# Attention with a routed mixture of experts on one core: the router's first choice queued one pair after its logits, the expert's number computed earlier in its round, half of the first expert's first matrix asked for after the first tokens are turned, and two penalty steps of round 0 on VectorE

## The chip, the core and the metric

The kernel runs on one core of a Trainium2 chip. The metric is the device time of one execution in microseconds (us). The engines have short names in the profile: PE is TensorE (its weight loads are PEld), DVE is VectorE, ACT is ScalarE, POOL is GpSimd and SP is SyncE. Each works through its own instructions in a fixed order and waits on semaphores. Here SP issues the plain DMAs, and GpSimd the indirect ones (gathers and scatters of rows).

## The reference

```python
# q, k, v: (8 batches, 8 heads, 576 positions, 64), fp32
scores = q @ k.T / sqrt(64) + bias(head, distance), inside a causal window of 128
x = (softmax(scores) @ v) as (4608 tokens, 512)
# mixture of experts: 8 experts, each takes at most cap = 576 tokens
logits = x @ w_gate                       # (4608, 8)
for idx in argsort(-logits.flatten()):    # greedy, best pair first
    tok, e = idx // 8, idx % 8
    if assigned[tok] < 0 and counts[e] < cap:
        assigned[tok] = e; counts[e] += 1
for e in range(8):
    out[assigned == e] = relu(x[assigned == e] @ w1[e]) @ w2[e]
```

## The kernel before

**Attention** (`attention`, L26). The work goes over 32 pairs of heads (4 pairs in each of 8 batches), in a software pipeline that is written out by hand: the loop at L316 has, for each `n`, the weights' minima of pair n-1 (`least`, DVE, L133) and their exponentials (`exps`, ACT), the transposes of pair n-2 on PE (`turn`, L157) with copies out of PSUM (`turned`, the tiles `PT`, L165), attention times values of pair n-3 (`av`, tile `x`, L53), and the end of pair n-4: `copy_out` (ACT, and one small GpSimd copy `xT<-xT`, L215), `natural` (PE, weights `wn`, tiles `pt`), and `divide` (DVE: a reciprocal `rs` at L240, shares of the logits `Lp` at L248, the output `xb` at L255). All of these are kept in program order on their engines. After the last pair of a batch, `logits` (L287) adds the shares up on GpSimd in four small adds (L296 to L299) into `L_sb`; for the last batch DVE does it itself (L291).

**The router** (`Router`). It replaces the greedy loop by eight rounds: in each one the expert that fills up first is settled, by counting how many candidates lie above each of 64 thresholds. Its work of round 0 is spread over the attention part as steps (generators): `first_choice` (best expert of each token, two steps: `b`, `ne`, `cand`, and then `am`, `OH`), put on a list by `early` (L595), and, after batch 5, `early_counts` (L618: `ext`, `em`, `ed`, then `ev` to `hi`, then `w` to `kq`, then the indicators `ind` and PE's counts). `early_step` (L607) runs one step a pair, at L363, behind `divide`. Since they are issued through a helper, these instructions all have line 442 in the profile (L446 in the changed program). The rest of round 0 (`phase`, L647) follows the attention: its results are `ei` (the expert's number, as an integer) and `idx` (the rows of its tokens).

**The handover** (`layer_moe`, L979). GpSimd gathers the first expert's tokens by `idx` (`g`, five gathers, L840). SP reads `ei` into a register and loads the first weight matrix in four quarters of 512 KB (`raw`, L822): three (`SOON`) at once, the last one after `late`, a copy of `ei` on DVE that is queued behind the first step of round 1. PE runs `WARM0` = 10 matmuls on zeros (L848) to be kept busy, then turns the tokens (`turn`, L851: tiles `pg` and `po` on PE, `xh` on ACT, `xl` on DVE) with `WARM1` = 4 matmuls on zeros behind each of the first two groups. Each quarter is split into a rounded part and the rest (`split`, L825: a cast `hl` on ACT, L829, and two subtractions on DVE, L831).

**The experts.** For each of eight experts: `layer1` (tile `ph`, L887, then relu on ACT and the rest on DVE) and `layer2` (tile `po`, L912 to L915), and a scatter of the rows by GpSimd. Expert 0 goes over the first 256 tokens for all eight column blocks, and then over the others; blocks 0 and 1 need quarter 0 of the matrix, blocks 2 and 3 quarter 1, and so on, 12 matmuls a block and token group. `slot` puts the next round's steps, weight loads, splits and gathers between the matmuls. From L984 on a scheduler sets the order on each engine, and `tc.issue_after(i)` only says that what is issued in the block stands behind instruction `i` on its own engine. In each round but the last, the candidates of the settled expert are struck out (`L2`, `Lt`, `L1` at L756 to L759, on GpSimd), and round k+1 begins with `first_choice` on the result.

Of the kernel before, what the change touches and what calls it, by code (L numbers as in the profile page):

```python
# [5 lines left out]
F32 = mybir.dt.float32  # L6
F32R = mybir.dt.float32r
BF = mybir.dt.bfloat16
I32 = mybir.dt.int32
AF = mybir.ActivationFunctionType  # L10
ALU = mybir.AluOpType
# [8 lines left out]
NT = N // 128  # L20
# [5 lines left out]
def attention(tc, pools, qk_in, v_in, rel_in, C, x_dram, L_sb, router):  # L26
# [289 lines left out]
    for n in range(NPAIRS + LAG + 2):  # L316
# [42 lines left out]
        if ends:  # L359
            divide(k - 2, N)  # L360
            if (k - 2) % NP == NP - 1 and k - 2 < NPAIRS - 1:
                logits((k - 2) // NP)
            router.early_step(room if turns else None)  # L363
        if 0 <= k - 1 < NPAIRS - 1:
            av(k - 1)
        if n < NPAIRS:
            scores(n, 1)
# [39 lines left out]
CONST_AT = 4  # L407
WARM, WARM0, WARM1 = 11, 10, 4
EARLY = 4
AHEAD = (18, 0, 0)  # L410
EARLY0 = 1
SOON, HI0 = 3, 1
W_LOAD = [(0, 1, 0, 0), (0, 1, 1, 2), (0, 1, 2, 6), (0, 1, 3, 10),
# [17 lines left out]
def bc(ap, shape):  # L431
    return ap.to_broadcast(shape)
# [17 lines left out]
class Router:  # L450
# [144 lines left out]
    def early(self, c0, c1):  # L595

        choice = self.first_choice(self.L0, self.b0, self.am0, self.OH0, c0, c1)
        if c1 == NT:
            for steps in self.steps + [choice]:
                for _ in steps:  # L600
                    pass
            return
        self.steps.append(choice)
        if c1 == FIRST:
            self.steps.append(self.early_counts())
# [12 lines left out]
    def early_counts(self):  # L618
# [6 lines left out]
        for i in range(EARLY_CUTS):  # L625
            a, z = (c1 * j // EARLY_CUTS for j in (i, i + 1))
            self.indicate(ind, key, a, z)
            if i % 2 == 1:
                yield
        cnt = self.count(ind, self.OH0, 0, c1)  # L630
# [16 lines left out]
    def phase(self, k, exact=False):  # L647
# [48 lines left out]
        nc.vector.scalar_tensor_tensor(keyv, Dc, float(CAP), self.left, ALU.is_ge, ALU.mult)  # L696
        nc.vector.tensor_reduce(mx, keyv, AX.X, ALU.max)

        m = rt.tile([128, NT], BF, name="m")
# [8 lines left out]
        nc.tensor.matmul(sp[:, 0:NT], self.C["tri"], m, start=False, stop=True)  # L708
        ef = self.small("ef")
        nc.vector.tensor_scalar(ef, mx, 1.0, -1.0, ALU.max, ALU.mult)  # L710
        ei = self.ei[k] = rt.tile([128, 1], I32, name="ei", bufs=4)
        nc.vector.tensor_scalar(ei, ef, 8.0, None, ALU.add)
        hi = self.small("hif", NT)
# [37 lines left out]
        if k < 7:  # L751
# [3 lines left out]
            L2 = rt.tile([128, 8, NT], F32, name="L2", bufs=1)  # L755
            self.tc.nc.gpsimd.tensor_tensor(L2, L, bc(self.pen.unsqueeze(2), [128, 8, NT]), ALU.add)  # L756
            Lt = rt.tile([128, 8, NT], F32, name="Lt", bufs=1)
            self.tc.nc.gpsimd.tensor_scalar(Lt, T1, 100.0 * BIG, 1.0, ALU.mult, ALU.mult)
            self.tc.nc.gpsimd.tensor_tensor(self.L1, Lt, L2, ALU.add)  # L759
        ov = self.small("ov")  # L760
# [50 lines left out]
class MoE:  # L811
# [39 lines left out]
    def turn(self, gs, first=False):  # L851
# [6 lines left out]
        for h, (g, r) in enumerate(gs):  # L858
# [6 lines left out]
            if first and h < TURN0 - 1:  # L865
                self.keep_warm(WARM1)
            nc.scalar.copy(xh[:, :, 128 * h:128 * h + r], ps[:, :, :r])  # L867
            nc.vector.tensor_tensor(xl[:, :, 128 * h:128 * h + r], ps[:, :, :r],  # L868
                                    xh[:, :, 128 * h:128 * h + r].bitcast(F32), ALU.subtract)
# [109 lines left out]
def layer_moe(tc, P, C, r, x, w1, w2, out, exact):  # L979
# [4 lines left out]
    with tc.issue_after(r.last.ins):  # L984
        for _ in range(EARLY0):
            next(route)
        late = P["rt"].tile([1, 1], I32, name="late")
        last = tc.nc.vector.tensor_copy(late, r.ei[0][0:1, 0:1])
    raw += list(m.loads(late, 0, range(SOON, 4)))
    W = {(0, 0): [m.split(raw[c]) for c in range(HI0)]}  # L990
# [4 lines left out]
    with tc.issue_after(m.last.ins):  # L995
        for _ in range(TURN0):
            next(tn)
# [130 lines left out]
```

## Time and profile before

| what | value |
|---|---|
| median of 3 runs | 739.1 us (739.07 to 739.36) |
| the profiled execution | 739.65 us |
| its span, first to last instruction | 737.8 us |
| PE busy | 682.8 us, 93% |
| PE weight loads busy | 599.2 us, 81% |
| DVE busy | 468.0 us, 63% |
| ACT busy | 331.4 us, 45% |
| POOL busy | 154.5 us, 21% |
| granted clock of PE, mean | 0.971 |
| moved by DMA | 92.74 MB |

The profile is one execution. The attention part fills the first 236 us or so, the rest of round 0 and the handover go to about 267 us, and the experts have what follows. In the timeline a row is: start, duration, engine, line, operation, out<-in, shape, count, and in brackets how long the engine stood idle before it and what ended that. In a table of windows each row is a stretch: its length, the busy time and the instructions of PE, PEld, DVE, ACT and POOL, the granted clock of PE, the busy share of the DMA engines and GB/s. The router's instructions in attention are told apart by their tiles, since all have line 442.

### The profile page before, as it was taken

To read this page: it belongs to the slowest core of one execution; us is meant where nothing else is said; L and a number is where in the kernel's file an instruction comes from. 1 tells how busy PE (TensorE), PEld (TensorE's weight loads), DVE (VectorE), ACT (ScalarE), POOL (GpSimd) and SP (SyncE) were. 2 spreads that over 40 slices of the span, in tenths; PEclk is the share of its full clock that TensorE was granted. 3 is DMA by queue.
4 is the path that set the end of the run, shared out by engine and by line. 5 is a ranking of instruction groups with operands and counts; after the bars stand their busy time and mean duration, and the time that the engine had idled before them with its cause. 6 is when DMAs were issued, how large, how long until landed. Compare 5 with 4: busy or idle time off the path is not lost.

```text
span 737.8 us, 19156 instructions
## 1 busy us (share of the span) xinstructions
PE 682.8 (93%) x7416; PEld 599.2 (81%) x7417; DVE 468.0 (63%) x1854; ACT 331.4 (45%) x990; POOL 154.5 (21%) x340
## 2 busy tenths in 40 slices
PE   7989889899897479999999999999999999999992
PEld 4888788788786268889878989988988988989981
DVE  6767678677777788969768847856865625423200
ACT  6878788688785152424223324314224324322200
POOL 4111221121212121323123132132033022011010
PEclk9999999999999599999999999999999999999996
DMA  8465465455522360815326135135134325201010
GB/s 298 136 201 170 139 194 170 156 174 173 154 84 81 112 203 1 290 60 183 131 88 228 44 130 157 58 124 174 60 115 148 117 93 169 76 29 36 1 36 32
DMA packets 35140, 92.74 MB, mean 126 GB/s; under 512 B 3808, under 2 KB 13152, under 8 KB 35040
## 3 DMA queue, kind: packets, MB, share of 16 engines
q1 hardware_dynamic: 29152, 72.55, 30.0%
q0 software_dynamic: 5888, 18.88, 7.8%
q8 instruction: 60, 0.98, 0.6%
q14 instruction: 40, 0.33, 0.1%
HBM read 72.54 MB, written 18.87 MB: 124 GB/s over the span
## 4 chain that ended last, share of the span: by engine, by line
PE 78%; DVE 13%; DMA 3%; POOL 2%; issue 2%; ACT 1%; SPq 0%; POOLq 0%; DVEq 0%; ACTq 0%
PE ph L887 25%; PE po L912 10%; PE po L913 10%; PE po L915 8%; PE s L53 6%; PE pt L53 5%; PE pt L157 4%; DVE u L133 4%; PE x L53 4%; PE pg L864 2%; PE m L575 1%; DMA craw<-in_cst_dram 1%; DVE PT L165 1%; DMA g<-x,idx 1%; DMA qk<-in_qk_dram 1%
## 5 line engine op out<-in xcount | busy, mean ns | idle before, releaser
L887 PE MATMUL ph<-xh,hl 128*128 128x288 f32 (+2 forms) x1024 | 191.8, 299 | 0.0
L887 PEld LDWEIGHTS ph<-xh,hl 128*128 128x128 f32 x1024 | 154.5, 189 | 1.0
L144 ACT ACTIVATE u<-u,mn 128x192 f32<-128x192 f32 (+2 forms) x288 | 123.9, 433 | 33.9 <-DVE mn L133 33.9
L912 PE MATMUL po<-hl,hh 128*128 128x512 f32 x320 | 129.4, 404 | 0.0
L913 PE MATMUL po<-hl,hh 128*128 128x512 f32 x320 | 124.9, 390 | 0.0
L887 PE MATMUL ph<-xl,hl 128*128 128x288 f32 (+2 forms) x512 | 115.8, 297 | 0.0
L893 ACT ACTIVATE hh<-ph 128x288 fp32r<-128x288 f32 (+2 forms) x128 | 46.4, 409 | 149.8 <-PE ph L887 140.8
L133 DVE CUSTOM_DVE_ANT_0 u<-s,bm 128x192 f32<-128x192 f32 x308 | 86.4, 333 | 41.2 <-PE s L53 40.7
L915 PE MATMUL po<-hl,hlo 128*128 128x512 f32 x256 | 100.3, 392 | 0.0
L831 DVE TENSOR_TENSOR hl<-raw,hl 128x512 fp32r<-128x512 f32 x128 | 85.4, 688 | 14.9 <-ACT hl L829 13.4
L928 POOL DMA_INDIRECT out_dram<-o,idx x40 | 44.5, 1112 | 204.6 <-ACT o L923 115.8
L887 PEld LDWEIGHTS ph<-xl,hl 128*128 128x128 f32 x512 | 84.2, 189 | 0.0
L868 DVE TENSOR_TENSOR xl<-pg,xh 128x512 fp32r<-128x512 f32 (+1 forms) x37 | 23.7, 640 | 84.7 <-ACT xh L867 84.5
L898 DVE SCALAR_TENSOR_TENSOR hlo<-ph,hh 128x288 fp32r<-128x288 f32 (+2 forms) x128 | 49.5, 417 | 40.8 <-ACT hh L893 40.0
L829 ACT CAST hl<-raw 128x1024 fp32r<-128x1024 f32 x64 | 65.5, 1049 | 19.7 <-DMA raw<-in_w_dram 14.7
L53 PE MATMUL s<-qk 64*64 64x192 f32 (+1 forms) x1112 | 70.1, 326 | 2.0 <-DVE mn L133 1.7
L157 PE MATMUL pt<-ident_sb,u 128*128 128x128 f32 x368 | 54.2, 282 | 17.0 <-DVE PT L165 15.6
L912 PEld LDWEIGHTS po<-hl,hh 128*128 128x128 f32 x320 | 60.2, 188 | 11.5
L913 PEld LDWEIGHTS po<-hl,hh 128*128 128x128 f32 x320 | 60.3, 188 | 11.1
L157 PEld LDWEIGHTS pt<-ident_sb,u 128*128 128x128 f32 x368 | 39.1, 140 | 27.7 <-DVE PT L165 18.4
L923 ACT COPY o<-po 128x512 f32<-128x512 f32 x31 | 18.2, 587 | 88.2 <-PE po L915 53.4
L840 POOL DMA_INDIRECT g<-x,idx x40 | 42.9, 1073 | 68.7 <-PE pg L864 33.8
(218 smaller groups left out, 951.9 us busy)
## 6 DMA issues: line engine op xcount, KB each, us to landing
raw<-in_w_dram SPq DMA_DIRECT2D x64, 512.0 KB, 3.5
qk<-in_qk_dram SPq DMA_DIRECT2D x32, 576.0 KB, 4.8
v<-in_v_dram SPq DMA_DIRECT2D x32, 288.0 KB, 3.4
x<-xb SPq DMA_DIRECT2D x14, 512.0 KB, 3.5
x<-xb SPq DMA_DIRECT2D x8, 128.0 KB, 3.0
x<-xb SPq DMA_DIRECT2D x4, 256.0 KB
g<-x,idx POOLq DMA_INDIRECT x40
out_dram<-o,idx POOLq DMA_INDIRECT x40
```

What stands on the lines that cost most here:

```text
L53: put(nc.tensor.matmul(out, w, a, start=start, stop=stop, skip_group_check=True))
L133: put(nc.vector.tensor_tensor_reduce(out=u[rows], in0=x[rows, c:c + 64 * m].rearrange("q (j k) -> q j k", k=64), in1=bm[n % NP][rows, y:y ...
L144: put(nc.scalar.activation(u, u, AF.Exp, bias=st["mn"][:, i:i + 1], scale=-1.0, accum_out=st["sm"][:, i:i + 1]))
L157: put(nc.tensor.transpose(ps[:, c:c + 128], u[:, o + 128 * j:o + 128 * j + 128], ident))
L829: self.last = nc.scalar.copy(hl[:, 0, :], raw)
L831: nc.vector.tensor_tensor(hl[:, 1, c:c + 512], raw[:, c:c + 512], hl[:, 0, c:c + 512].bitcast(F32), ALU.subtract)
L887: nc.tensor.matmul(pp[t], w[:, a, j, fo:fo + 128], x[:, j, cut[t]:cut[t + 1]], start=(j == 0 and a == 0 and x is xh), stop=(j == 3 and a = ...
L893: nc.scalar.activation(o, pp[t], AF.Relu)
L898: nc.vector.scalar_tensor_tensor(d, pp[t][:, c0:c1], 0.0, o[:, c0:c1].bitcast(F32), ALU.max, ALU.subtract)
L912: nc.tensor.matmul(po, a, wh, start=(f == 0), stop=False)
L913: nc.tensor.matmul(po, a, wl, start=False, stop=(f == 7 and t == 4))
L915: nc.tensor.matmul(po, hl[:, f, 128 * t:128 * t + 128], wh, start=False, stop=(f == 7))
```

## The change

1. `early` puts an empty step in front of each batch's `first_choice`, so the choice begins one pair after its logits were added up; all router steps behind it move by a pair too. From pair 32 of the loop on, the step runs behind `av` and not before it, and twice where nothing is turned any more. `early_counts` issues its three indicators in one step.
2. `ef` and `ei` stand directly behind `kmx`, before `m`.
3. In round 0 the penalties `L2` and `L1` are computed on DVE, `L1` in one operation without `Lt`. The other rounds are as before.
4. `SOON` is 2: two quarters are loaded by `ei`, the other two by `late`, which now stands behind the first turned tokens (`m.turned`, an `xl`). `WARM0` is 16.

```diff
-            router.early_step(room if turns else None)
+            if n < NPAIRS:
+                router.early_step(room)
         if 0 <= k - 1 < NPAIRS - 1:
             av(k - 1)
+        if n >= NPAIRS:
+            for _ in range(1 if turns else 2):
+                router.early_step(room if turns else None)
...
-WARM, WARM0, WARM1 = 11, 10, 4
+WARM, WARM0, WARM1 = 11, 16, 4
...
-SOON, HI0 = 3, 1
+SOON, HI0 = 2, 1
...
-        self.steps.append(choice)
+        self.steps += [iter([None]), choice]
...
             self.indicate(ind, key, a, z)
-            if i % 2 == 1:
-                yield
...
         nc.vector.tensor_reduce(mx, keyv, AX.X, ALU.max)
+        ef = self.small("ef")
+        nc.vector.tensor_scalar(ef, mx, 1.0, -1.0, ALU.max, ALU.mult)
+        ei = self.ei[k] = rt.tile([128, 1], I32, name="ei", bufs=4)
+        nc.vector.tensor_scalar(ei, ef, 8.0, None, ALU.add)
...
-        ef = self.small("ef")
-        nc.vector.tensor_scalar(ef, mx, 1.0, -1.0, ALU.max, ALU.mult)
-        ei = self.ei[k] = rt.tile([128, 1], I32, name="ei", bufs=4)
-        nc.vector.tensor_scalar(ei, ef, 8.0, None, ALU.add)
...
-            self.tc.nc.gpsimd.tensor_tensor(L2, L, bc(self.pen.unsqueeze(2), [128, 8, NT]), ALU.add)
-            Lt = rt.tile([128, 8, NT], F32, name="Lt", bufs=1)
-            self.tc.nc.gpsimd.tensor_scalar(Lt, T1, 100.0 * BIG, 1.0, ALU.mult, ALU.mult)
-            self.tc.nc.gpsimd.tensor_tensor(self.L1, Lt, L2, ALU.add)
+            eng = nc.vector if k == 0 else self.tc.nc.gpsimd
+            eng.tensor_tensor(L2, L, bc(self.pen.unsqueeze(2), [128, 8, NT]), ALU.add)
+            if k == 0:
+                nc.vector.scalar_tensor_tensor(self.L1, T1, 100.0 * BIG, L2, ALU.mult, ALU.add)
+            else:
+                Lt = rt.tile([128, 8, NT], F32, name="Lt", bufs=1)
+                eng.tensor_scalar(Lt, T1, 100.0 * BIG, 1.0, ALU.mult, ALU.mult)
+                eng.tensor_tensor(self.L1, Lt, L2, ALU.add)
...
-            nc.vector.tensor_tensor(xl[:, :, 128 * h:128 * h + r], ps[:, :, :r],
+            self.turned = nc.vector.tensor_tensor(xl[:, :, 128 * h:128 * h + r], ps[:, :, :r],
...
         for _ in range(EARLY0):
             next(route)
-        late = P["rt"].tile([1, 1], I32, name="late")
-        last = tc.nc.vector.tensor_copy(late, r.ei[0][0:1, 0:1])
-    raw += list(m.loads(late, 0, range(SOON, 4)))
...
     tn = m.turn(g, True)
     with tc.issue_after(m.last.ins):
-        for _ in range(TURN0):
+        next(tn)
+
+    with tc.issue_after(m.turned.ins):
+        late = P["rt"].tile([1, 1], I32, name="late")
+        last = tc.nc.vector.tensor_copy(late, r.ei[0][0:1, 0:1])
+    raw += list(m.loads(late, 0, range(SOON, 4)))
+    with tc.issue_after(m.last.ins):
+        for _ in range(TURN0 - 1):
             next(tn)
```

On DVE in attention, at the end of the pair whose batch has just been completed, and of the pair behind it (`L442` and `L446` are the helper's line before and after the change):

```order
 L255 TENSOR_TENSOR xb<-pt,rs 128x2x128
-L442 TENSOR_REDUCE b_73<-L_sb 128x4
-L442 TENSOR_TENSOR ne<-L_sb,b_73 128x8x4
-L442 SCALAR_TENSOR_TENSOR cand<-ne,c_eb 128x8x4
 L133 ISA u,mn<-s,bm_300 128x3x64
...
 L255 TENSOR_TENSOR xb<-pt,rs 128x2x128
-L442 TENSOR_REDUCE am_75<-cand 128x4
-L442 TENSOR_TENSOR OH_76<-c_eb,am_75 128x8x4
+L446 TENSOR_REDUCE b_73<-L_sb 128x4
+L446 TENSOR_TENSOR ne<-L_sb,b_73 128x8x4
+L446 SCALAR_TENSOR_TENSOR cand<-ne,c_eb 128x8x4
 L133 ISA u,mn<-s,bm_119 128x2x64
```

The three ops that read `L_sb` have left the pair in which it is written and stand where `am` and `OH` stood; those two stand one pair further on.

On GpSimd at the handover, before the change (`g` are the gathers, `L_4822` is `L2` and `L_72` is `L1`):

```order
L215 COPY xT<-xT 128x64 x2
L758 TENSOR_SCALAR Lt<-T_4754 128x288
L840 DMA g<-x,idx 128x512
L756 TENSOR_TENSOR L_4822<-L_sb,pen 128x288
L840 DMA g<-x,idx 128x512
L759 TENSOR_TENSOR L_72<-Lt,L_4822 128x288
L840 DMA g<-x,idx 128x512 x2
L840 DMA g<-x,idx 64x512
```

and after it:

```order
L219 TENSOR_SCALAR sd<-sm 128x8
L222 TENSOR_SCALAR sd<-sm 64x1 x4
L215 COPY xT<-xT 128x64 x2
L846 DMA g<-x,idx 128x512 x4
L846 DMA g<-x,idx 64x512
L764 TENSOR_SCALAR Lt<-T_5283 128x288
```

The five gathers stand together, with nothing of round 0 between them.

On DVE at the same place, after the change, from `idx` to the second group of turned tokens (`hl` are the splits' subtractions, `L_72` is `L1`):

```order
L446 TENSOR_TENSOR L_4822<-L_sb,pen 128x288
L837 TENSOR_TENSOR hl<-raw,hl 128x512
L446 SCALAR_TENSOR_TENSOR L_72<-T_4754,L_4822 128x288
L446 TENSOR_REDUCE ov<-Dc 128x1
L837 TENSOR_TENSOR hl<-raw,hl 128x512
...
L837 TENSOR_TENSOR hl<-raw,hl 128x512
L493 SCALAR_TENSOR_TENSOR cand<-ne,c_eb 128x288
L874 TENSOR_TENSOR xl<-pg,xh 128x4x128
L495 TENSOR_REDUCE am<-cand 128x36
L1003 COPY late<-ei 1x1
L874 TENSOR_TENSOR xl<-po,xh 128x4x128
```

Before, `late` stood behind `left` and one `ov`, ahead of all splits; now it stands behind four subtractions (two quarters) and the first `xl`.

## Prediction

> **What bounds the kernel now.** I first read the span and asked which waits TensorE (PE) has in the attention part. The columns are total, times, longest, in us; the rows are PE's own longest wait and the waits that stand behind it on VectorE (DVE).
>
> ```profile
> span 737.8 us, 19156 instructions
> ...
> PE pt L157 <- DVE PT L165: 15.6, 12, 2.1
> ...
> DVE b L442 <- POOL L_sb L299: 5.4, 3, 1.8
> DVE b L442 <- POOL L_sb L298: 4.6, 3, 1.5
> ```
>
> PE loses 15.6 us waiting for DVE copies (`PT`), and DVE itself stands 10.0 us, in six places, before the first op of `first_choice` (`b`), whose logits GpSimd has not yet added up. The timeline shows one of the six.
>
> ```profile
> 187.66 1.58 PE L53 MATMUL x<-PT,v 64*64 64x64 f32 x68
> ...
> 192.34 0.23 DVE L442 TENSOR_REDUCE b<-L_sb 128x5 f32<-128x40 f32 x1 [1.81 <-POOL L_sb L299]
> 192.37 0.24 POOL L215 COPY xT<-xT 128x64 f32<-128x64 f32 x1
> ...
> 192.66 0.30 PEld L53 LDWEIGHTS pt<-wn_sb,xT 128*128 128x128 f32 x2 [0.26 <-POOL xT L215]
> 192.84 0.21 DVE L442 SCALAR_TENSOR_TENSOR cand<-ne,c_eb 128x40 bf16<-128x40 bf16 x1
> ...
> 195.31 0.44 PE L157 MATMUL pt<-ident_sb,u 128*128 128x128 f32 x2 [2.14 <-DVE PT L165]
> ...
> 196.67 2.73 PE L53 MATMUL x<-PT,v 64*64 64x64 f32 x68
> ```
>
> DVE stands 1.81 us, then does 0.7 us of choice (192.34 to 193.05); everything queued behind it on DVE is late by that sum, the `PT` copy too, and PE stands 2.14 us. Then the same 68 matmuls take 2.73 us in place of 1.58. The windows say why; the column after POOL is PE's granted clock. The first eight windows run from one `rs` reciprocal (L240, one a pair) to the second after it: six that hold a stall, two that hold none.
>
> ```profile
> 46.52:62.67 16.15, 14.16 (x255) 12.68 (x254) 10.97 (x62) 11.32 (x45) 3.56 (x16) 0.89 0.49 153
> 75.65:91.38 15.73, 13.28 (x278) 11.70 (x276) 10.95 (x62) 11.19 (x45) 3.68 (x16) 1.00 0.49 157
> 103.85:119.00 15.15, 12.93 (x255) 11.42 (x254) 10.90 (x62) 11.19 (x45) 3.56 (x16) 1.00 0.52 163
> 131.98:148.59 16.61, 14.43 (x277) 13.04 (x276) 11.04 (x60) 11.27 (x45) 3.67 (x16) 0.90 0.46 149
> 161.06:176.19 15.13, 12.92 (x255) 11.42 (x254) 10.88 (x60) 11.19 (x45) 3.55 (x16) 1.00 0.52 164
> 189.18:205.78 16.60, 14.41 (x263) 12.57 (x265) 11.22 (x64) 11.31 (x45) 3.67 (x16) 0.90 0.47 150
> 91.38:103.85 12.47, 12.47 (x260) 11.46 (x258) 9.86 (x57) 11.07 (x45) 2.37 (x12) 1.00 0.59 187
> 119.00:131.98 12.98, 12.98 (x273) 11.54 (x272) 10.12 (x57) 11.08 (x45) 2.38 (x12) 1.00 0.57 180
> ...
> 196.90:200.20 3.30, 3.30 (x82) 3.22 (x76) 2.92 (x17) 2.54 (x10) 1.08 (x6) 0.50 0.03 7
> ```
>
> Two plain pairs take 12.7 us on the mean, with PE busy throughout; two with a stall take 15.1 to 16.6. The six sum to 95.4, six plain ones to 76.4: 19.0 us of excess. Three of the six have the clock at half for a while (0.89, 0.90, 0.90), and are on the mean 1.1 us longer than the three at 1.00.
>
> The other loss is the handover to the experts, the last part that I read.
>
> ```profile
> 250.91 0.15 DVE L442 TENSOR_SCALAR ei<-ef 128x1 int32<-128x1 f32 x1
> ...
> 252.10 18.47 SPq L822 DMA_DIRECT2D raw<-in_w_dram  x8
> ...
> 254.60 3.92 PE L848 MATMUL ph<-zero 128*128 128x512 bf16 x9 [0.22 <-issue]
> ...
> 254.84 0.33 DVE L442 SCALAR_TENSOR_TENSOR idx<-ia 64x5 int32<-64x5 f32 x2
> ...
> 256.14 1.19 POOL L840 DMA_INDIRECT g<-x,idx  x1 [7.05 <-DVE ov L442]
> 257.36 0.92 POOL L756 TENSOR_TENSOR L<-L_sb,pen 128x288 f32<-128x288 f32 x1
> 259.69 0.80 POOL L759 TENSOR_TENSOR L<-Lt,L 128x288 f32<-128x288 f32 x1
> 262.09 1.11 PE L864 MATMUL pg<-ident_sb,g 128*128 128x128 f32 x4 [3.57 <-DMA g<-x,idx]
> 264.25 0.68 DVE L868 TENSOR_TENSOR xl<-pg,xh 128x512 fp32r<-128x512 f32 x1
> 266.02 1.05 ACT L829 CAST hl<-raw 128x1024 fp32r<-128x1024 f32 x1
> 266.67 0.72 PE L887 MATMUL ph<-xh,hl 128*128 128x256 f32 x4
> 268.20 1.89 DVE L831 TENSOR_TENSOR hl<-raw,hl 128x512 fp32r<-128x512 f32 x3
> ```
>
> The first gather is issued at 256.14 and its tokens are there at 262.09, 5.95 us later; PE, warmed until about 259, stands 3.57 us, and the first expert matmul follows at 266.67.
>
> ```profile
> 257.90:261.70 3.80, 0.62 (x2) 0.00 (x0) 2.11 (x4) 1.27 (x2) 3.37 (x4) 0.95 0.91 290
> 261.70:265.10 3.40, 3.01 (x10) 1.86 (x11) 3.40 (x9) 0.59 (x1) 2.37 (x2) 0.50 0.83 275
> 487.90:489.60 1.70, 1.70 (x9) 1.39 (x8) 0.23 (x1) 0.00 (x0) 1.00 (x1) 1.00 0.00 0
> ```
>
> While that gather flies, the DMA engines are 91% busy with weights, and after PE's wait the clock is at half for 3.4 us. The third row holds a lone gather of a later expert: nothing moves for 1.70 us after its issue, so its 256 KB, at the 290 GB/s of the first row, would be there after about 2.6 to 3.
>
> **The change part by part.** *First choice one pair later.* In the pair after the logits the step is now empty, and GpSimd has a whole pair (over 6 us) for the adds that DVE waited 1.81 us for. DVE's wait goes in all six places, and with it the 2.1 us waits of PE after which the clock fell. What stays: the same five ops of choice, 0.7 us for the three shown and at most as much for the other two, on a DVE that PE waits for, so 0.6 to 1.1 us an event; and a wait that DVE's stall has covered so far. GpSimd's `xT` copy (192.37) still stands behind the four adds, and PE's last two `wn` weight loads wait for it until 192.66. They would have come at about 191.9; but PE's next work needs a `PT` copy, which without the stall could be done at 192.7, so this costs some 0.25 us, at most 0.8. I take 1.2 us of 3.2 as staying: 6 x 1.2 = 7.4, so 11.6 of 19.0 go. Bounds: all but 0.6 an event goes, 15.4; or 0.8 and 1.1 stay and the half clock too (3 x 1.1 = 3.3), 19.0 - 11.4 - 3.3 = 4.3.
>
> The Trainium skill ("TensorE: Matmul & The Clock Gate", "What's actually happening") has the clock halved after an idle window of about 3.4 us. Here a wait of 2.14 us sufficed, so the measurement decides; by the page's rule the stall would not be the cause, 3.3 us of half clock would stay, and the time would be 727.4.
>
> *The other router steps move one pair later too.* Of them `w` to `kq` leaves a pair in which PE waits for DVE, for one after the last scores.
>
> ```profile
> 221.03 0.20 DVE L442 TENSOR_SCALAR w<-hi,lo 128x1 f32<-128x1 f32 x1
> ...
> 222.36 0.31 DVE L442 TENSOR_SCALAR kq<-c,lo,rw 128x52 bf16<-128x52 f32 x1
> ...
> 230.57 0.32 PE L442 MATMUL pt<-OH,ind 128*128 128x16 bf16 x5 [0.32 <-DVE ind L442]
> ```
>
> That is 1.6 us of DVE (221.03 to 222.67), and the 0.32 us for which PE stood before `av` goes because counts now follow `av`. From the sum of 1.9 I take 1.5, since 1.6 us of DVE may push the `PT` copies of pair 31; bounds 0 and 1.9. Folding the indicator steps together removes a step and no work.
>
> *Expert number sooner.* Its two small ops stand before `m` in place of behind `ex`: three DVE ops stand no longer before `ei`, which I put at half a microsecond, and `idx` comes some 0.3 later (two dependent ops of 0.15, as the `ei` row), so the gather would be issued at 256.45 in old time.
>
> *Penalties on DVE, two quarters of the weights late.* Now 1 MB and not 1.5 is on its way before the gathers, half a microsecond sooner, and the five gathers follow each other on GpSimd without the 0.92 and 0.80. The tokens are then there 2.9 us after 256.45, at 259.4; at worst as now, 262.4. PE's 16 warm-up matmuls, 0.436 us each at half clock (3.92 for 9), begin at 254.9 and end at 261.9 if the clock never rises, at 260.0 if half of them run at full. I take 260.9 for the first transposes: here the warm-ups, not the gather, decide. From there to the first expert matmul before took 4.58 us (262.09 to 266.67), 3.0 of them at half clock; at full clock about 3.4. So 264.3 in place of 266.7: 2.4 us. Bounds: 260.0 and 3.1 give 263.1, 3.6 gained; 262.4 and 4.6 give 267.0, 0.3 lost.
>
> The cover for the late quarters:
>
> ```profile
> raw<-in_w_dram SPq DMA_DIRECT2D x64, 512.0 KB, 3.5
> ...
> 271.15 5.47 PE ph L887 x44
> ```
>
> The first `xl` (2.16 us behind its transposes at half clock) starts at about 262.3 and ends at 263.0, `late` follows after one op (put at 0.6, as one of the three subtractions) at 263.6, the DMA is issued 1.2 later, as after `ei` (250.91 to 252.10), and lands 3.5 later, at 268.3; cast 1.05, the first half's subtraction 0.63: the third quarter is usable at 270.0. PE needs it after 48 matmuls of 0.124 us, at 270.3. The slack is 0.3 us; a landing of 5 us would cost 1.2. SP's queue is held by `late` until then, and behind it only second-layer loads stand, which aren't needed before some 23 us of layer 1. PE's waits inside the first expert I expect about 0.5 us longer, since its counts of the next round now stand earlier in PE's row; bounds -0.6 and 1.9, one subtraction less or three more in front of them.
>
> The Trainium skill ("SBUF — State Buffer", "Who interferes with whom") speaks against this edit: GpSimd, which writes a gather's descriptors, is locked out of their shared port by some DVE instructions, and DVE now has more to do at this point. The gather of 256.14 took 1.19 us and the lone one 1.00 (busy POOL in its window): 0.2 us at most, and the rule stays as a rival.
>
> **The sum.** -11.6 - 1.5 - 2.4 + 0.5 = -15.0 us. The profiled execution took 739.65 us (span 737.8 and 1.85 around it), which gives 724.65; the median of the runs is 0.55 lower, 739.1, so 724.1.
>
> **The rivals.** (1) *The handover gives nothing:* the warm-ups stay cold, or the third quarter comes 2 to 3 us late. For it: a slack of only 0.3 us. Against: 91% busy DMA was what held the gather. 739.1 - 11.6 - 1.5 + 0.5 = 726.5, chance 0.14. GpSimd held off by DVE, by one 0.63 us subtraction for each of the first three gathers, gives 726.0; chance 0.04. Half clock that comes in attention without the stall, 3.3 us, gives 727.4; chance 0.03, since the three longest events are those that have it. (2) *The wait moves to GpSimd:* PE stands the whole 0.8 us for `xT` in each event, and the clock still falls. For it: 0.26 us of that wait is in the trace. Against: it's at most a third of the 2.14 us after which the clock fell. The gain of the first edit becomes 4.3 to 8: 739.1 - 6 - 1.5 - 1.9 = 729.7; chance 0.07. (3) *Slower:* PE starves in the first expert's first layer while it waits for late quarters, and its clock stays at half, as it did from 261.70 to 265.10. A window of 3.4 us at half costs 1.7 us of PE's work, so it decides from nine windows in a row, 15.3 us, which gives 739.4 and more with PE's waits on top, 741. The layer is long enough (192 matmuls at 0.124 us, 24 us at full clock); but PE would have to stand much of every window, and only two quarters are late. Chance 0.01. (4) *It doesn't do what it says:* the steps are kept in program order, and the order shows them moved; 739, chance 0.01. The forecast has 0.70.
>
> **How the numbers follow.** Forecast 724.1, its own range 720.5 to 727.5 (the handover's bounds and 0.4 us an event). Rival 2 widens it upward to 730; downward, 15.4 and 3.6 both coming give 719. I say 719.5 to 730. About 0.2% (1.5 us) is what a measurement of this kernel can tell from no change: faster 0.97, same 0.015, slower 0.015.
>
> **What would show it.** Right: no DVE wait for `L_sb`; windows over two pairs after logits of 13.5 to 14.3 us at clock 1.00; the first expert matmul 2.4 us nearer to `idx`; the first gather there within 3.5 us. Wrong: PE waits for `xT` of over 0.5 us, clock under 1 in attention, PE waits for `hl` in the first layer, or warm-ups that end after the gather has landed by more than 2 us.

## The result, and the profile after

The kernel after the change takes 721.7 us (median of 4 runs, 721.6 to 722.3), the kernel before, beside it on the same chip, 739.2 us (4 runs): a ratio of 0.9765, 95% interval 0.9748 to 0.9781, 17.5 us less. The profiled execution took 722.27 us. Single executions of the kernel before, in the rounds of the experiments below, lie between 737.2 and 743.9 us (mean granted clock 0.975 and 0.964), so a difference of one or two us between two of them says little.

The waits in the attention part, in the same columns as before (total, times, longest, in us):

```profile
core 0 of [0], span 720.5 us
...
PE pt L157 <- DVE PT L165: 6.2, 14, 0.9
...
PEld pt L53 <- POOL xT L215: 0.8, 3, 0.3
```

DVE's waits for `L_sb` are gone from the list. PE's wait for `PT` copies fell from 15.6 to 6.2 us, the longest from 2.1 to 0.9. No row has PE itself waiting for GpSimd's `xT`; only its weight loader does, 0.8 us in all.

One of the six places in the timeline of after, the pair that now holds the first half of the choice:

```profile
188.19 0.22 DVE L446 TENSOR_REDUCE b<-L_sb 128x5 f32<-128x40 f32 x1
...
188.69 0.21 DVE L446 SCALAR_TENSOR_TENSOR cand<-ne,c_eb 128x40 bf16<-128x40 bf16 x1
...
191.02 0.44 PE L157 MATMUL pt<-ident_sb,u 128*128 128x128 f32 x2 [0.51 <-DVE PT L165]
...
192.38 1.58 PE L53 MATMUL x<-PT,v 64*64 64x64 f32 x68
```

The choice no longer waits, costs the 0.71 us of its three ops (188.19 to 188.90), and PE stands 0.51 us in place of 2.14; the 68 matmuls behind take 1.58 us again, not 2.73.

The windows of after, cut at the same reciprocals (the first six rows: the two pairs behind each of six batches' logits; the last two: the next two pairs behind the first two of these); the column behind POOL is PE's granted clock:

```profile
47.87:61.08 13.21, 12.70 (x255) 11.42 (x254) 10.51 (x60) 11.09 (x45) 3.53 (x16) 1.00 0.62 187
74.39:88.00 13.61, 13.05 (x277) 11.68 (x276) 10.53 (x60) 11.18 (x45) 3.66 (x16) 1.00 0.59 181
100.82:114.02 13.20, 12.69 (x255) 11.41 (x254) 10.50 (x58) 11.08 (x45) 3.53 (x16) 1.00 0.60 187
127.34:140.95 13.61, 13.06 (x278) 11.68 (x276) 10.53 (x60) 11.18 (x45) 3.65 (x16) 1.00 0.59 181
153.77:166.97 13.20, 12.69 (x255) 11.41 (x254) 10.49 (x58) 11.08 (x45) 3.53 (x16) 1.00 0.58 188
180.29:193.90 13.61, 13.05 (x277) 11.68 (x276) 10.53 (x60) 11.17 (x45) 3.66 (x16) 1.00 0.58 182
61.08:74.39 13.31, 13.05 (x273) 11.54 (x272) 10.42 (x59) 11.07 (x45) 2.35 (x12) 1.00 0.56 175
88.00:100.82 12.82, 12.56 (x260) 11.46 (x258) 10.18 (x57) 11.07 (x45) 2.36 (x12) 1.00 0.57 182
```

The six sum to 80.4 us against 95.4, all at clock 1.00. The last two, plain before, now hold the choice's second half, and each took 0.34 us more than before. An event is therefore counted over three pairs below: 134.0 us before for the six, 120.8 after.

The handover in after (timelines of DVE, PE, GpSimd and the DMA queue):

```profile
237.57 0.15 DVE L446 TENSOR_SCALAR ei<-ef 128x1 int32<-128x1 f32 x1
...
242.16 5.35 PE L854 MATMUL ph<-zero 128*128 128x512 bf16 x15 [0.22 <-issue]
...
242.39 0.33 DVE L446 SCALAR_TENSOR_TENSOR idx<-ia 64x5 int32<-64x5 f32 x2
...
243.69 1.18 POOL L846 DMA_INDIRECT g<-x,idx  x1 [22.18 <-ACT hl L835]
...
247.34 0.60 PE L870 MATMUL pg<-ident_sb,g 128*128 128x128 f32 x4
...
249.75 0.13 DVE L1003 COPY late<-ei 1x1 int32<-1x1 int32 x1
...
250.66 2.34 SPq L828 DMA_DIRECT2D raw<-in_w_dram  x4
...
250.75 0.60 PE L893 MATMUL ph<-xh,hl 128*128 128x256 f32 x3
...
256.02 1.29 DVE L837 TENSOR_TENSOR hl<-raw,hl 128x512 fp32r<-128x512 f32 x2
```

The first transposes start 3.65 us behind the first gather's issue (5.95 before), with no gap between them and the warm-ups, and the first expert matmul 3.41 us later (4.58 before). The late quarters are issued at 250.66, and the third is split from 256.02 on; PE shows no wait for it.

Where the 17.29 us of the two spans went, stage by stage (us, from the timelines; a minus is time gained):

| stage | predicted | measured |
|---|---|---|
| six events, three pairs each | -11.6 | -13.2 |
| last pairs, to the last logits sum | -1.5 | -0.9 |
| `idx` later / gather to transposes / transposes to first expert matmul | -2.4 | +0.3 - 2.3 - 1.2 = -3.2 |
| experts, to the end | +0.5 | -1.4 |
| up to the first pair's reciprocal | 0 | +1.4 |

The last row belongs to that one execution: there is nothing of the change in that stretch, and the start of the other kernels' profiles below varies by as much. The four rows of the change add up to -18.7, against -15.0 in the forecast.

### The profile page after: what moved, and what is told of

Read it like the earlier page. It is cut to its first block, busy times and chain, and to the rows that moved or that the text cites. A ratio compares the mean times of both kernels' runs of the same rounds, so it can differ in the third digit from the quotient of the medians.

```text
span 720.5 us, 19162 instructions
## 1 busy us (share of the span) xinstructions
PE 678.5 (94%) x7422; PEld 595.2 (83%) x7423; DVE 466.9 (65%) x1856; ACT 330.6 (46%) x990; POOL 155.2 (22%) x337
## 4 chain that ended last, share of the span: by engine, by line
PE 80%; DVE 14%; DMA 2%; issue 1%; SPq 0%; ACT 0%; POOL 0%; POOLq 0%; DVEq 0%; ACTq 0%
PE ph L893 28%; PE po L918 10%; PE po L919 10%; PE po L921 8%; PE s L53 6%; DVE u L133 5%; PE pt L53 5%; PE pt L157 4%; PE x L53 3%; PE pg L870 2%; DVE xb L255 2%; PE m L579 1%; DMA craw<-in_cst_dram 1%; DVE PT L165 1%; PE ph L854 1%
## 5 line engine op out<-in xcount | busy, mean ns | idle before, releaser
L837 DVE TENSOR_TENSOR hl<-raw,hl 128x512 fp32r<-128x512 f32 x128 | 85.0, 683 | 14.3 <-ACT hl L835 13.9
L846 POOL DMA_INDIRECT g<-x,idx x40 | 44.8, 1120 | 82.0 <-PE pg L870 33.9
L921 PEld LDWEIGHTS po<-hl,hlo 128*128 128x128 f32 x256 | 48.0, 188 | 10.6
```

Of the source, the lines that this page charges most:

```text
L837: nc.vector.tensor_tensor(hl[:, 1, c:c + 512], raw[:, c:c + 512], hl[:, 0, c:c + 512].bitcast(F32), ALU.subtract)
L921: nc.tensor.matmul(po, hl[:, f, 128 * t:128 * t + 128], wh, start=False, stop=(f == 7))
```

## The experiments

My theory: nearly all of the gain is the wait that DVE no longer has for GpSimd's sum, with the PE waits and the half clock that follow from it (some 13.5 us); the handover brings some 3. Rivals: the choice is merely in a better place, the wait did not matter; or the handover and the clock carry the gain; or DVE's new work holds off GpSimd's gathers and hides a larger gain.

All the runs in one table; before is the median beside them on the same chip. "Events" is the sum over six times three pairs; then the times from the first gather's issue to the first transposes, from these to the first expert matmul, and from this to the last matmul, all from one profile of each kernel.

| kernel | median us | before | ratio, 95% interval | events | gather to transposes | to first matmul | experts |
|---|---|---|---|---|---|---|---|
| before | | 739.2 | | 134.0 | 5.95 | 4.58 | 457.1 |
| after | 721.7 | 739.2 | 0.9748 to 0.9781 | 120.8 | 3.65 | 3.41 | 455.8 |
| attention_alone | 724.5 | 739.5 | 0.9758 to 0.9832 | 120.9 | 5.76 | 4.86 | 456.3 |
| no_empty_step | 736.1 | 739.5 | 0.9937 to 0.9981 | 133.9 | 3.60 | 3.37 | 456.2 |
| logits_on_dve | 730.5 | 739.5 | 0.9844 to 0.9932 | 124.3 | 5.51 | 5.77 | 455.8 |
| penalties_on_gpsimd | 726.7 | 739.5 | 0.9784 to 0.9868 | 120.9 | 4.08 | 4.51 | 459.3 |
| three_quarters_first | 723.5 | 739.2 | 0.9754 to 0.9812 | 120.8 | 4.11 | 3.29 | 458.8 |
| ten_warmups | 726.2 | 739.2 | 0.9775 to 0.9838 | 120.9 | 4.13 | 4.80 | 459.0 |
| two_groups_turned | 726.0 | 739.2 | 0.9782 to 0.9842 | 120.9 | 4.03 | 2.85 | 459.7 |
| choice_once_per_two | 719.7 | 739.2 | 0.9710 to 0.9767 | 118.9 | 3.64 | 3.39 | 455.8 |
| steps_before_av | 724.7 | 739.4 | 0.9763 to 0.9828 | 120.8 | 3.59 | 3.35 | 456.7 |
| choice_once_per_three | 719.0 | 739.4 | 0.9683 to 0.9739 | 118.3 | 3.99 | 3.36 | 456.6 |
| two_inputs_beside_gathers | 725.1 | 739.4 | 0.9752 to 0.9841 | 120.9 | 3.63 | 3.38 | 458.9 |
| one_input_beside_gathers | 725.7 | 739.4 | 0.9763 to 0.9846 | 120.9 | 3.74 | 3.34 | 460.3 |

**The attention edits alone** (before with these lines of the change and nothing else):

```
-            router.early_step(room if turns else None)
+            if n < NPAIRS:
+                router.early_step(room)
...
+        if n >= NPAIRS:
+            for _ in range(1 if turns else 2):
+                router.early_step(room if turns else None)
...
-        self.steps.append(choice)
+        self.steps += [iter([None]), choice]
...
-            if i % 2 == 1:
-                yield
```

> Only the attention edits (empty step ahead of each first choice, later router steps, step behind av from pair 32 on, indicators in one step); the handover as before. My theory (the gain in attention is DVE's six waits for GpSimd, PE's waits behind them and the half clock that they bring): the attention part is 13 to 14 us shorter, the handover as before, 725.5 us (724.5 to 726.5). Rival (the handover and a better phase of the clock carry much of the 17.5 us): 729 or more.

724.5 us. Events as in after, handover as in before (GpSimd's first three gathers stand 2.4 and 2.2 us apart, PE waits for the first):

```profile
247.59 1.11 PE L866 MATMUL pg<-ident_sb,g 128*128 128x128 f32 x4 [3.30 <-DMA g<-x,idx]
```

These edits alone bring 15.0 of the 17.5 us. By the profile, 14.1 of them lie in the attention part (13.2 in the events, 0.9 in the last pairs) and 0.8 in the experts, which these edits leave alone. The handover as the carrier of the gain is out.

**The empty step alone taken away** (after with one element less):

```
-        self.steps += [iter([None]), choice]
+        self.steps.append(choice)
```

> The changed kernel without the empty step: the first choice stands again in the pair of its logits, all other edits stay. My theory: the six DVE waits, 10 us, and the half clock come back; what is left is the handover, 3.5 us, and 1.4 us of waits inside the experts: 734.3 us (733.3 to 735.5). Rival (what helps is that steps moved to cheaper places around the last pairs): 726 or less.

736.1 us, 0.6 above the expected range (the profiled execution, 734.99, lies in it). The waits of this kernel in attention are those of before, to the digit:

```profile
PE pt L157 <- DVE PT L165: 15.6, 12, 2.1
...
DVE b L446 <- POOL L_sb L299: 5.4, 3, 1.8
...
DVE b L446 <- POOL L_sb L298: 4.6, 3, 1.5
```

One empty element in a list of steps is worth 13 us; the events are back at 133.9, and three of them have windows at half clock.

**The wait taken away, the choice left in its old place** (before with the sums of all batches on DVE, as the last batch has them, so that no GpSimd result is waited for):

```
-        if b == B - 1:
+        if b >= 0:
```

> The kernel before, with the logits of every batch added up on DVE in two reductions, as the last batch has it, in place of GpSimd's four adds; the first choice stays in the same pair. My theory (it is the wait, not the place): no wait and no half clock, but 0.64 us more work on DVE in each of seven pairs and the choice's work as before; of the 19.0 us of excess some 9 to 11 remain, so 729 to 731 us, 730. Rival (it is the place: the pair of the logits can't take the choice's work): the excess stays, 736 to 739 us.

730.5 us. The events fall by 9.8 us although DVE has more to do in that pair, and the clock stays at 1.00 in attention in the profiled execution. PE's waits in that part lie between; the second fence has the last event, 23.33 us long before:

```profile
PE pt L157 <- DVE PT L165: 11.1, 15, 1.6
```

```profile
181.02:202.46 21.44, 19.38 (x390) 16.83 (x391) 17.08 (x95) 16.75 (x67) 3.56 (x18) 1.00 0.49 154
```

So most of it is the wait, not the place. What is left against after is 3.4 us. The sums that GpSimd did beside DVE are six times 0.62 us on DVE here, 3.7 us, so they could be all of it; this kernel doesn't separate them from the place of the choice.

**The penalties of round 0 back on GpSimd** (after with these two lines):

```
-            eng = nc.vector if k == 0 else self.tc.nc.gpsimd
+            eng = self.tc.nc.gpsimd
...
-            if k == 0:
+            if k < 0:
```

> The changed kernel with round 0's penalties on GpSimd again, in three operations as before. My theory (the second and third gather set the first expert matmul once the first is early): the gathers stand apart again, the third 1.6 us later, the first expert matmul 1 to 1.6 us later: 722.9 us (722.3 to 723.5). Rival (DVE's added work holds the gathers or the splits up as much as it saves): 721.7 us or less.

726.7 us, well above what I expected. The handover lost 1.5 us, as expected; the timelines of GpSimd and PE:

```profile
242.18 1.62 POOL L846 DMA_INDIRECT g<-x,idx  x1 [7.30 <-ACT hl L835]
243.84 0.68 POOL L759 TENSOR_TENSOR L<-L_sb,pen 128x288 f32<-128x288 f32 x1
244.68 1.23 POOL L846 DMA_INDIRECT g<-x,idx  x1 [0.17 <-issue]
...
246.26 0.66 PE L870 MATMUL pg<-ident_sb,g 128*128 128x128 f32 x4 [0.56 <-DMA g<-x,idx]
...
297.16 0.66 PE L870 MATMUL pg<-ident_sb,g 128*128 128x128 f32 x4 [2.08 <-DVE xl L874]
```

But the last row lies some 46 us into the experts, where the second expert's tokens are turned: there PE now waits 2.08 us, the clock falls to half behind it, and the experts take 3.5 us longer. The two edited lines do not touch this place, but the order of the instructions on DVE, ACT and PE is another there than in after. The profiles below fall into two groups, with this loss and without it.

**Three quarters of the first matrix ahead of the gathers, not two** (after with `SOON, HI0 = 3, 1`):

> After, with three quarters of expert 0's first matrix in flight ahead of the gathers instead of two. My theory (the gather lands behind the weights that are already moving): 512 KB more are ahead of it, so the first gather takes 1.6 to 2.3 us longer to the first transposes (3.65 us in after becomes 5.3 to 5.9, as the 5.76 of the run with the attention edits alone), the time is 723.2 to 724.0. Rival (only the spacing of GpSimd's descriptors matters, the bytes in flight do not): transposes stay 3.6 to 3.8 us behind the gather's issue, 721.7.

723.5 us, in my range for the wrong reason. The gather took 4.11 us to the transposes, 0.46 longer than in after and not 1.6 to 2.3, and even that is no price: ten_warmups and choice_once_per_three, with two quarters ahead, have 4.13 and 3.99. The time went in the second expert's turn, 3.0 us. My step, "1 MB and not 1.5 is on its way before the gathers", is not what freed the gather. The DMA queue's rows in before (from one window of its timeline) show what did:

```profile
256.42 2.88 SPq L822 DMA_DIRECT2D raw<-in_w_dram  x2
```

Before, a fourth and a fifth quarter were issued at 256.42 and 258.96, while the gather of 256.14 was in flight. After, and in this experiment, the queue is held by `late` until the first tokens are turned, and issues nothing in that time. So it is the place of `late`, not the number of quarters, that matters; what the earlier `ei` adds was not separated (the first quarter is issued 4.0 us ahead of the gather before, 4.9 in this experiment and in after). The gathers' closeness counts for the groups behind the first: with the penalties between them PE waited 0.51 and 0.44 us for the second and third, and the stretch to the first expert matmul was 1.1 us longer.

**Ten warm-ups, not sixteen** (after with `WARM, WARM0, WARM1 = 11, 10, 4`):

> After, with 10 warm-up matmuls of TensorE ahead of the first transposes instead of 16. In after the warm-ups ran without a gap into the transposes. My theory (warm-ups, not the gather, decide by a little): they end 1 to 2 us sooner, the transposes then come as soon as the gather has landed, 0.2 to 0.8 us sooner, and the clock still rises at the same place: 721.0 to 721.5. Rival A (the gather decides already): transposes at the same place, 721.7. Rival B (the gap of idle TensorE keeps the clock at half): transposes to the first expert matmul 4.5 us or more instead of 3.4, 722.8 or more.

726.2 us: my theory fell, rival B holds. Timeline of PE, and two windows of this kernel:

```profile
240.71 3.28 PE L854 MATMUL ph<-zero 128*128 128x512 bf16 x9 [0.22 <-issue]
246.38 1.05 PE L870 MATMUL pg<-ident_sb,g 128*128 128x128 f32 x4 [2.38 <-DMA g<-x,idx]
```

```profile
243.10:246.50 3.40, 1.01 (x5) 0.32 (x4) 3.40 (x12) 0.10 (x1) 2.70 (x3) 1.00 0.43 102
246.50:249.90 3.40, 3.40 (x13) 2.23 (x14) 1.44 (x4) 0.58 (x1) 1.86 (x2) 0.50 0.70 212
```

The gather is there 4.13 us after its issue, so PE stands 2.38 us with nothing to do, and the transposes behind run at half clock: 4.80 us to the first expert matmul. The six warm-ups that were added cost nothing, since they end about when the tokens come, and save 1.4 us by the clock. (The other 3 us are again in the second expert's turn.)

**Two groups of tokens turned before the first expert matmul, not three** (after with `TURN0 = 2`):

> After, with two groups of 128 tokens turned before the first expert's matmuls instead of three. My theory (what lies between the first transposes and the first expert matmul is TensorE's own row: transposes and warm-ups of the third group): the first expert matmul starts 0.7 to 1.4 us sooner, 2.0 to 2.7 us behind the first transposes instead of 3.41, and the time is 720.4 to 721.2 if the third group's tokens are there in time. Rival (the first half of the matrix, cast and subtracted, decides): 3.4 us as now, 721.7.

726.0 us. The first matmul came 0.56 us sooner, less than the 0.7 to 1.4 I expected; PE then waited 2.6 us for `ind` in the second expert's turn, and the experts took 3.9 us longer:

```profile
PE m L579 <- DVE ind L555: 2.6, 1, 2.6
```

**The router's steps of the last pairs ahead of the context matmuls** (after with the loop's order as before, the empty step kept):

```
-            if n < NPAIRS:
-                router.early_step(room)
+            router.early_step(room if turns else None)
...
-        if n >= NPAIRS:
-            for _ in range(1 if turns else 2):
-                router.early_step(room if turns else None)
```

> After, with the router's steps of the last pairs (those without scores of their own) back ahead of the context matmuls, as in before; the empty step stays. My theory: the move after the last scores is worth the 0.5 us that the last five reciprocals show between before and after (23.13 to 22.62) and the 0.36 us behind them, 0.5 to 0.9 us together: 722.2 to 722.6. Rival (the 1.5 us of the prediction is there, but elsewhere, in the summing-up behind the last pair): 723.2 or more. Rival (the move is worth nothing): 721.7.

724.7 us, with an interval too wide to size the step; the profile does: 0.9 us up to the last reciprocal, 0.1 and 0.3 behind it, 1.3 in all, more than the 0.5 to 0.9 I expected (0.9 more lies in the experts). The row that makes it:

```profile
217.76 1.05 PE L442 MATMUL pt<-OH,ind 128*128 128x16 bf16 x13 [0.96 <-DVE ind L442]
```

With the choice one pair later and the loop's order unchanged, PE would wait 0.96 us for the indicators, where before it waited 0.32. The reordering is what keeps the first edit from costing this. Part of the wait may come from the indicators, which this kernel issues in one step and the kernel before in two; no run separates that.

**The first choice once for two, and once for three batches** (after with these lines in `early`; the second kernel with `c1 not in (13, 27)` and `c0 = {13: 0, 27: 13}[c1]`):

```
+        if c1 <= FIRST:
+            if c1 % 9:
+                return
+            c0 = c1 - 9
```

> After, with the first choice (which expert each token prefers) taken once for two batches of logits in one step, where after takes it for each batch by itself. If what is left in the three pairs around each logits batch (20.0 to 20.4 us against 6.5 us a pair undisturbed, about 0.6 to 0.9 us an event) is DVE's first choice standing ahead of the copies TensorE waits for, half of the choices' cost goes in three events but the other three are twice as long for element-wise steps: 0.3 to 0.6 us an event gained where there is none, little lost in the others, 719.3 to 721.0. Rival (what is left is the logits' own matmuls and GpSimd's copy): 721.7. Rival (a choice twice as long makes TensorE wait long enough for half clock): clock 0.5 windows in attention, 723 to 725.

> After, with the first choice taken once for three batches of logits. An event costs 0.90 us with the choice of one batch (20.02 against 19.12 without) and 1.27 us with that of two (20.39), so by a straight line 1.64 us with three: six events come to 114.72 + 3.28 = 118.0 against 118.89, and the time is 719.2 at 0.9 us less than 719.7 would be 718.8. Rival (three batches at once make a stall that TensorE waits for): an event of 21 us or more, or half clock, and 720.5 or more.

719.7 and 719.0 us, both as my theory has it (events 118.9, and 118.3 where 118.0 was expected). Windows over three pairs of the second kernel, one without and one with a choice:

```profile
46.27:65.40 19.13, 19.13 (x388) 17.19 (x387) 15.04 (x84) 16.63 (x67) 4.75 (x22) 1.00 0.64 202
97.37:117.96 20.59, 19.26 (x388) 17.17 (x387) 16.41 (x87) 16.74 (x67) 4.75 (x22) 1.00 0.57 188
```

Without a choice PE is busy for the whole of its 19.13 us; with three batches at once it loses 1.46. So what after still pays in these pairs, 0.9 to 1.1 us an event, is the choice's own DVE ops, and by the straight line through 0.90 us for one batch and 1.27 for two, an estimate, half a microsecond of it comes with each choice whatever its size (three batches cost 1.46 and 1.66, where the line has 1.64). The last, 0.9711 (0.9683 to 0.9739) of before, is the best here, below after's interval; that of choice_once_per_two overlaps it.

**Does DVE's work hold off the gathers?** In after one gather of the second expert took 3.26 us on GpSimd, while DVE did one subtraction behind the other:

```profile
286.81 3.26 POOL L846 DMA_INDIRECT g<-x,idx  x1 [0.31 <-issue]
```

Two kernels add idle work on DVE right behind the first expert's `idx`, whose results nothing uses:

```
+            two = rt.tile([128, 8, NT], F32, name="two", bufs=1)
+            for _ in range(8):
+                nc.vector.tensor_tensor(two, L, L, ALU.add)
```

and, in its place, six `tensor_reduce(one, L, ..., ALU.max)`.

> After, with eight idle additions on DVE in the row behind expert 0's indices, each of two operands in SBUF (128x288 of float32, result not used), which interleave with the subtractions of the first quarters, so that DVE runs two-operand work without a gap while GpSimd issues the five gathers. Theory A (such DVE work holds off GpSimd's gather, as the gather of 3.26 us beside 3.35 us of subtractions in after suggests): at least one gather takes 2.5 us or more on GpSimd, the first transposes come 2 us later or more, 724 or more. Theory B (the long gather has another reason, the DMA queue's own room): all five take 0.9 to 1.7 us, transposes 3.6 to 4.2 us behind the issue, 722 to 723, or 725 if the row of expert 1's turn falls out as in the runs that lost 3 us there.

> After, with six idle reductions on DVE at the same place, each of one operand in SBUF (0.63 us). DVE is as full as with the eight additions, but half of its time without a second operand. Theory A: every gather finds room between two subtractions, 0.9 to 1.9 us each, the transposes 3.6 to 4.3 us behind the issue. Theory B: the same. Theory C (any DVE work holds off GpSimd): gathers as long as in the run with the additions. Time 722 to 725.

GpSimd and DVE in the first of them:

```profile
241.99 1.19 POOL L850 DMA_INDIRECT g<-x,idx  x1 [22.15 <-DMA raw<-in_w_dram]
243.48 1.03 POOL L850 DMA_INDIRECT g<-x,idx  x1 [0.30 <-issue]
...
241.99 0.72 DVE L841 TENSOR_TENSOR hl<-raw,hl 128x512 fp32r<-128x512 f32 x1 [0.48 <-ACT hl L839]
242.63 0.45 DVE L446 TENSOR_TENSOR two<-L_sb 128x288 f32<-128x288 f32 x1
243.00 0.68 DVE L841 TENSOR_TENSOR hl<-raw,hl 128x512 fp32r<-128x512 f32 x1
```

From 241.99 to 245.99 DVE runs two-operand work without a gap, and the three gathers in that time take 1.19, 1.03 and 1.03 us (the last two, with gaps on DVE, under 1.0); with the reductions all five take 0.92 to 1.24. Theory A is out for these gathers, and with it the rival that DVE's new work hides part of the gain; why that one gather took 3.26 us stays open. Both kernels lost 3 to 4.5 us in the second expert's turn.

That loss sorts the runs: the experts take 455.8 to 457.1 us in eight kernels and 458.8 to 460.3 in the other six, and the difference lies nearly all between 26 and 67 us behind the first expert matmul, where the second expert's weights and tokens arrive together. PE waits there 1.0 to 2.7 us at a time, for `ind`, `xl` or a gather, and in some of them the clock falls too.

The six are just those that edit the handover of after. The other eight have the handover of before or of after unchanged. In no_empty_step, one of the eight, DVE's 176 instructions of the 64 us that begin 2 us behind the first expert matmul stand in the same order as in after; in the profiles of the six they stand in another. So the loss seems to come with the order that the scheduler gives the second expert's turn once the handover is edited; which order brings it was not separated. Nor is it known that every execution of such a kernel has it: those of ten_warmups took 722.4 to 726.8 us. The medians of these six therefore don't price their edits, only the stage times do. No run takes the earlier `ei` or the three indicators in one step alone.

## Why the prediction was right, step by step

The forecast was 724.1 us, the result 721.7, within the range; the direction and the main cause held. All four terms were off, by 1.6, 0.6, 0.8 and 1.9 us. Together they are 3.7 us short of the gain, of which the later start of the profiled execution hides 1.4: that the total came so close is in part luck.

- **Six events, -11.6, measured -13.2.** The mechanism is shown from three sides: without the wait and in the old place (logits_on_dve) most of the excess goes, without the empty step all of it is back, with the attention edits alone all of it is there. The excess was sized right (19.0; 134.0 less three times 19.13 and three times 19.25, the events without a choice in choice_once_per_three, gives 18.9). The windows over two pairs, 13.2 to 13.6 us, lie at the lower end of the 13.5 to 14.3 that I gave as a sign of being right. What stays is 0.95 us an event, not 1.2: the 0.25 us for PE's wait on `xT` did not come. The sum had a slip, too: six times 1.2 is 7.2 and not 7.4, so the term was -11.8 by its own figures and the forecast 723.9.
- **Half clock, 3.3 us.** It went with the stall, in the profiles of after, attention_alone and logits_on_dve, and came back with it in no_empty_step. The rival that it has another cause is out.
- **The wait moves to GpSimd.** It did not: the weight loader's 0.8 us in all is what is left of it. The rows gave no ground for the 0.8 us an event that I set as the bound: the loader stood 0.26 us before 192.66, so the loads would have come at 192.40, not 191.9.
- **Last pairs, -1.5, measured -0.9.** The step that failed: "`w` to `kq` leaves a pair in which PE waits for DVE". It did, but the step ahead of it in the list moved into that pair, and PE's wait there fell only from 1.30 to 0.94 us:

```profile
208.65 0.15 DVE L446 COPY ev<-pt 128x2 f32<-128x2 f32 x1
...
209.59 0.32 DVE L446 TENSOR_TENSOR hi<-ev,sp 128x1 f32<-128x1 f32 x1
...
212.06 0.55 PE L157 MATMUL pt<-ident_sb,u 128*128 128x128 f32 x3 [0.94 <-DVE PT L165]
...
216.40 0.49 PE L157 MATMUL pt<-ident_sb,u 128*128 128x128 f32 x3
```

  In these rows of after, 1.26 us of DVE (208.65 to 209.91) stand ahead of the `PT` copies that PE waits for at 212.06. My worry that `kq` would push the last pair's copies was unfounded: PE's next transposes of that kind (216.40) have no wait.
- **Handover, -2.4, measured -3.2.** Right: `idx` 0.26 later (0.3 expected), warm-ups run into the transposes, 3.41 us from these to the first expert matmul (3.4 expected). Off: the transposes came 0.8 us sooner than I put them. The warm-ups took 5.18 us (242.16 to 247.34), near the 5.1 of my lower bound and not the 6.0 that I took, as the clock was at full from 246.10. That moment is chance (it lies 0.2 us behind the gather's issue in choice_once_per_three), but it matters little: where the warm-ups end sooner PE waits for the gather, and the transposes come 3.6 to 4.1 us behind its issue in all eleven kernels with the new place of `late`. These are the rows of after:

```profile
242.70:246.10 3.40, 3.40 (x10) 1.16 (x9) 3.08 (x12) 2.02 (x2) 2.11 (x2) 0.50 0.23 58
246.10:249.50 3.40, 3.40 (x21) 1.83 (x20) 3.05 (x9) 0.62 (x2) 2.49 (x4) 1.00 0.65 201
```

  The term was also wrong in its reason: not fewer quarters ahead of the gathers but none beside them (three_quarters_first).
- **The third quarter.** Its slack of 0.3 us held: the first part of it is split at about 256.7 (half of the last row of the handover), the 48 matmuls ahead of it end at 256.7 by 0.124 us each from 250.75, somewhat later with the router's few between them, and PE shows no wait. The rival that this handover gives nothing is out.
- **Experts, +0.5, measured -1.4.** The sign was wrong. The waits inside the experts fell rather than rose; but attention_alone, whose experts are before's, has 456.3 and not 457.1, so that 0.8 us of this is no effect of the moved counts.
- **The range.** My own range was added up wrongly at its upper end: the handover's 2.7 us and 0.4 us an event above 724.1 give 729.2, not 727.5. The stated range of 719.5 to 730 covers both.

## What to carry to other kernels

An op that waits for another engine's slow sum delays everything queued behind it on its own in-order engine, and the price is paid by the engine behind that one; a pause of one loop turn in the queue of steps was worth more here (13.2 us) than moving the sum to the engine that waits for it (9.8 us). Look at what moves into the freed place, since in a list of steps each one takes its predecessor's. And judge an edit at a handover by its own stretch of the trace: all six kernels here that edited the handover of after lost 3 to 4.5 us in a later stretch, whose lines they did not touch.

## What the runs showed of the hardware

In the six stalls of before, whether the clock falls goes with where the wait lies. Windows of before, twice two that adjoin; the second column is the window's length, PE's busy time stands next, the clock behind POOL:

```profile
50.10:53.50 3.40, 1.45 (x29) 1.12 (x29) 2.47 (x14) 2.57 (x11) 0.00 (x0) 0.99 0.94 300
53.50:56.90 3.40, 3.40 (x86) 3.32 (x78) 2.71 (x15) 2.49 (x11) 0.95 (x5) 0.50 0.07 23
...
77.40:80.80 3.40, 2.20 (x17) 1.77 (x15) 1.90 (x14) 1.52 (x6) 1.39 (x5) 1.00 0.83 259
80.80:84.20 3.40, 2.41 (x80) 2.25 (x84) 2.02 (x9) 1.94 (x8) 0.00 (x0) 1.00 0.54 199
```

The stretches at half clock begin at 53.5, 138.8 and 196.8, which are 25 and 17 times 3.41 us apart, and each lasts 3.41 us: the clock is set on a fixed grid. In three stalls 1.9 to 2.2 us of idle time fall within one window of this grid, and the next window is at half clock; in the second pair above the grid cuts the wait in two (idle 1.2, then 1.0) and the clock stays. So three of six like stalls cost 1.1 us more than the others. The Trainium skill ("TensorE: Matmul & The Clock Gate", "What's actually happening") has a free-running window of 3413 ns, which agrees, and speaks of an idle window as what throttles; here a window with 1.45 us of work in it was enough. It is no sharp bound: one window with 1.25 us idle (three_quarters_first, in the second expert's turn) was followed by half clock, one with 1.99 us idle (two_inputs_beside_gathers, at the end of attention) was not. What else decides stays open.

The Trainium skill ("SBUF — State Buffer", "Who interferes with whom") has two-operand DVE work contend with GpSimd where GpSimd reads SBUF, and takes it as inferred that it doesn't stop the writing of descriptors. The gathers of 1.03 to 1.19 us beside gapless two-operand work agree with the second.
